# Decay attention and a hard-swish layer on one core: the exponent's bias folded into the reduction, the second layer's low weights from TensorE, and the last short unit spread over the last tile

## The chip, the cores and the metric

One core of a Trainium2 chip runs the whole program. The metric is device time in microseconds (us); lower is better. The engines are named as in the profile: PE (TensorE matmul), PEld (its weight load), DVE (VectorE), ACT (ScalarE), POOL (GpSimd) and SP (SyncE, which here issues the DMAs).

## The reference

Causal attention with a cumulative log decay for 8 batches of 8 heads (sequence 576, head size 64), then a two-layer network with a hard swish on the 4608 resulting rows (model size 512, inner size 2048), all in float32:

```python
scores = scale * np.matmul(q, k.transpose(0, 1, 3, 2))
cum = np.cumsum(np.log(np.clip(f, 0.0001, 1.0)), axis=-1)
scores = np.where(causal, -1000000000.0, scores + cum[:, :, :, None] - cum[:, :, None, :])
attn = np.exp(scores - np.max(scores, axis=-1, keepdims=True))
attn = attn / (np.sum(attn, axis=-1, keepdims=True) + 1e-09)
x = np.matmul(attn, v)          # heads side by side: 4608 x 512
h = x @ w_in                    # 512 x 2048
g = h * np.clip(h + 3.0, 0.0, 6.0) / 6.0
out = g @ w_out                 # 2048 x 512
```

## The kernel before, in words

**Precision.** Float32 products are made of float16 pieces. A matrix is scaled by a power of two and split into a high part (rounded to float16) and a low part (what is left), and a product is high x high, high x low and low x high, accumulated in PSUM. So the layers have three matmuls per block (L775 to L777 and L797 to L799 for the first, L821 to L823 for the second).

**Attention.** Batch 0 is worked on first, in pairs of heads cut at column 256 ("A" and "B" in `VH`). The 56 heads of batches 1 to 7 ("F") go through `rows`. For each of the two halves of a head's query chunks (`NAT`: three chunks, then two), `rows` computes the scores on PE into `pn` (L609, L612); DVE adds the causal mask and takes the maximum of each row in one pass (L620), writing the scores to `pp` and the maxima to `mc`; a small DVE pass turns the maxima into the exponent's bias `nb`, -max/8 + ln 16 (L626); ACT takes the exponential in place (L632), so that probabilities come out times 16 (`PSC`); ACT rounds them to float16 (L646), DVE or POOL subtract to get the low part (L649, L655, L660), and a transposing DMA brings both to `pT` (L667). `PL_POOL` and `B0_POOL` say which subtractions go to POOL: in batch 1 the chunk 3 piece of each head (L649); from batch 2 on the 64-column edges (L655, L660). `av` multiplies `pT` by the split values into `pav` (L692 to L697), and normalizes by the row sums (L721 to L727).

**POOL.** It rounds queries and keys for PE and makes their remainders (L447, L448, L456, L459).

**The layers.** A tile is 512 rows of one batch. `h_unit` makes 128 inner columns of the first layer: 12 matmuls into one PSUM bank `ph`, then ACT (L781), DVE (L784), ACT (L785) and DVE (L786) make the hard swish and its high and low part in `gT`. `out_unit` makes 128 output rows: 48 matmuls into `po`, an ACT pass (L827) and a DMA. The 64 rows by which a batch exceeds a tile are gathered for two batches into a short unit: `h_short` makes a quarter of its first layer (four groups of 128 columns, L797 to L812). For the last two batches the short unit is worked on within the last tile, in `gs`. `mm_tile` hands out the PSUM banks for all of these: two banks of the pool `ps_m`, and as every third, where its argument allows, the one bank "tr" of `ps_t`. Tile 0 comes in two parts, columns 0 to 255 and 256 to 511.

**The weights.** `w_in_work` and `w_out_work` load each weight in 16 chunks, sum its squares for a scale, and split it (`w_split`). For three of w_in's four groups the low part comes from PE: the chunk against an identity scaled by minus the scale (`eye`), plus the identity times the high part, evacuated by ACT with sign (L287 to L289). For w_out it comes from DVE (L295), which reads the float32 chunk and the high part that ACT has made (L284). The float32 of w_out's chunk k lies in the slot of `w2` that takes the parts of chunk k + 1.

**Order.** The main loop walks over `VH`; between a head's steps `fill` issues units of the layers at a rate (`F_RATE`, `even`) and `w_step` issues steps of the weights' work. That gives the program's order; the order on each engine is then made by a planner that simulates the engines with its own costs and takes the first in the program's order that it holds ready. Engines execute their queue in that order.

Of the kernel before, what the change touches and what calls it, by code (L numbers as in the profile page):

```python
# [20 lines left out]
def kernel(  # L21
# [79 lines left out]
    NSP = 3  # L101
    PL_POOL = ((3, ), ())
    NAT = ((1, 4, 0), (2, 3))
    B0_POOL = ((0, 0), (1, 1))
    W_AHEAD = (4, 5)
# [176 lines left out]
    def w_split(i, k, sc, eye=None):  # L282
        _, x, (hi, lo) = w_chunk(i, k)
        nc.scalar.activation(hi, x, AF.Copy, scale=sc)  # L284
        if eye is not None:
            pl = ps_m.tile([P, TT], F32, tag="mm", name=f"low_{k}")
            nc.tensor.matmul(pl, eye, x, start=True, stop=False)  # L287
            nc.tensor.matmul(pl, ident16, hi, start=False, stop=True)
            nc.scalar.activation(lo, pl, AF.Copy, scale=-1.0)  # L289
            return  # L290
        if POOL_REST[i][k % 4]:
            nc.scalar.activation(x, x, AF.Copy, scale=sc)
            nc.gpsimd.tensor_tensor(lo, x, hi, op=ALU.subtract)
        else:
            nc.vector.scalar_tensor_tensor(lo, x, sc, hi, op0=ALU.mult, op1=ALU.subtract)  # L295
# [29 lines left out]
    def w_out_work():  # L325
# [19 lines left out]
        for k in range(NW):  # L345
            w_split(1, k, scol(SW2 + k // NG))
            yield
# [242 lines left out]
    ringh = [t.bitcast(F16) for t in ring]  # L590

    def rows(v):
        i, j = v % NQK, v % NL
        n = VH[v][1]
        late = min(n // H, 2) - 1
        pT = p2.tile([P, 3200], F16, tag="PHL", name=f"pT_{v}")
        mc = MF[v % 2]
        nb = p2.tile([P, NCH], F32, tag="nb", name=f"nb_{v}")
        e0 = 0
        for half in range(2):  # L600
# [16 lines left out]
            for x, c in enumerate(NAT[half]):  # L617
# [3 lines left out]
                    pp[:r, w:w + kw], pn[:r, o:o + kw], W[:r, 4 * P + r - kw:4 * P + r],  # L621
                    1.0, -3.0e38, ALU.add, ALU.max, accum_out=mc[:r, e0 + x:e0 + x + 1],
                )
                w += kw
            e1 = e0 + len(NAT[half])
            nc.vector.tensor_scalar(  # L626
                nb[:, e0:e1], mc[:, e0:e1], -0.125, math.log(PSC), op0=ALU.mult, op1=ALU.add
            )
            for x, c in enumerate(NAT[half]):
                r, kw = RR[c], RB[c] + RR[c]  # L630
                x_ = pp[:r, at[c]:at[c] + kw]
                nc.scalar.activation(  # L632
                    x_, x_, AF.Exp, bias=nb[:r, e0 + x:e0 + x + 1], scale=0.125
                )
# [9 lines left out]
            for c in NAT[half]:  # L644
                r, kw, a = RR[c], RB[c] + RR[c], GH[half][c]
                nc.scalar.copy(hl[:r, h0[c]:h0[c] + kw], pp[:r, at[c]:at[c] + kw])  # L646
                if c:
                    eng = nc.gpsimd if c in PL_POOL[late] else nc.vector
                    eng.tensor_tensor(  # L649
                        hl[:r, a:a + c * P], pp[:r, at[c] + 64:at[c] + kw],  # L650
                        hl[:r, h0[c] + 64:h0[c] + kw], op=ALU.subtract,
                    )
            eng = nc.gpsimd if B0_POOL[late][half] else nc.vector
            a, b = NAT[half][:2]
            eng.tensor_tensor(  # L655
                pair(hl, h0[a] - 64, h0[b] - 64), pair(pp, at[a], at[b]), pair(hl, h0[a], h0[b]),
                op=ALU.subtract,
            )
            if 0 in NAT[half]:
                eng.tensor_tensor(  # L660
                    hl[:64, h0[0] - 64:h0[0]], pp[:64, at[0]:at[0] + 64], hl[:64, h0[0]:h0[0] + 64],
                    op=ALU.subtract,
                )
# [16 lines left out]
    def av(v, ph):  # L680
# [33 lines left out]
        for head in heads:  # L714
# [5 lines left out]
            rs = p2.tile([P, NCH, 1], F32, tag="rs", name=f"rs_{v}_{jh}")[:, p0:p1]  # L720
            nc.vector.tensor_scalar(  # L721
                rs, pav[:, p0:p1, vo + D:vo + D + 1], PSC * 1e-9, None, op0=ALU.add
            )
            nc.vector.reciprocal(rs, rs)
            if b == 0:
                nc.vector.tensor_scalar(rs, rs, scol(SV + b), None, op0=ALU.mult)
            nc.vector.tensor_tensor(  # L727
# [40 lines left out]
    def h_unit(t, fc, c0, c1):  # L768
        x = xT[t % 2]
        nw = c1 - c0  # L770
        ph = mm_tile(f"ph_{t}_{fc}_{c0}", t > 0 or c0 > 0)[:, :nw]
        fs_ = slice(fc * P, (fc + 1) * P)
# [59 lines left out]

    def moe_tile(t, c0=0, c1=TT):
        for fc in range(NFC):
            j, new = divmod(fc, NFC // NG)
            if new == 0 and c0 == 0:
                while j not in w_in_done:
                    next(w_in_q, None)
                moe_scale_in(t, j)
            yield from h_unit(t, fc, c0, c1)  # L840
        if t == 0:
            for _ in wq:
                pass
        if c0 == 0:
            moe_scale_out(t)
        last = t == B - 1
        if last:
            gs = vst.bitcast(F16).rearrange("p c e -> p (c e)")[:, 0:2 * NFC * P]
            gs = gs.rearrange("p (a f t) -> p a f t", a=2, f=NFC)
            for j in range(NG):  # L850
                yield from h_short(t // 2, j, gs)
        r0 = t * S + (64 if t else 0)
        for s in range(c0 // P, c1 // P):
            yield from out_unit(s, t > 0 or s * P >= QA, UO + t, [r0 + s * P])
        if last:
# [219 lines left out]
```

## Time and profile before

| | |
|---|---|
| median of 3 runs | 1076.95 us (1076.81 to 1079.76) |
| the profiled execution's own time | 1080.35 us |
| its span, first to last instruction | 1078.6 us |
| busy: PE, DVE, ACT, POOL | 1013.8, 726.8, 587.9, 408.5 us |
| mean granted PE clock | 0.985 |

Durations in this document come from the profiled execution; its own time is 1.75 us above its span and 3.40 us above the median. In the rows of the profile, a group of instructions is given as line, engine, operation, what it writes and reads, shapes and count, then its busy time in us and the mean ns of one, then the engine's idle time just before and which instruction ended it. Matmuls are pipelined: the duration of one includes its latency, and the distance from one start to the next is what it takes of PE. In rows of a timeline the first number is the start in us from the beginning of the span, the second the time it lasted.

### The profile page before, as it was taken

Reading aid. Unit: us, or ns where it says so; the run is one execution under the profiler, and the core shown is the slowest. Engines: PE = TensorE matmul, PEld = TensorE weight load, DVE = VectorE, ACT = ScalarE, POOL = GpSimd, SP = SyncE. Lnnn points to the kernel's source line nnn. Section 1 sums busy time; section 2 is a strip of 40 time slices with the busy share of each in tenths; the row PEclk is TensorE's granted clock in tenths of the full one; section 3 lists DMA queues with packets and bytes.
Section 4 is the critical chain, followed back from the end, with each engine's and each line's share of the span. In section 5 each row is a group of like instructions: output and inputs, shape, how many; then the busy total and the mean of one; then the engine's idle time right before and its main releaser. Section 6 shows DMA issues by size and latency. Waiting matters only on the chain.

```text
span 1078.6 us, 21257 instructions
## 1 busy us (share of the span) xinstructions
PE 1013.8 (94%) x7698; PEld 604.8 (56%) x7698; DVE 726.8 (67%) x1903; ACT 587.9 (55%) x1190; POOL 408.5 (38%) x505
## 2 busy tenths in 40 slices
PE   2799988899999999999999999999999999999897
PEld 2557854665455755555555755555555755544545
DVE  7887899887875668866865677767855678305300
ACT  4777657665664557555654547655743567315301
POOL 7434456454433445443434334443433442000000
PEclk9989989999999999999999999999999999999999
DMA  8976448965665676567465576567565554300000
GB/s 253 288 210 199 117 103 160 203 149 127 149 104 121 138 151 128 111 151 160 98 127 107 105 164 129 118 137 169 101 112 123 108 101 84 78 30 1 1 20 30
DMA packets 259300, 133.79 MB, mean 124 GB/s; under 512 B 226964, under 2 KB 228812, under 8 KB 259196
## 3 DMA queue, kind: packets, MB, share of 16 engines
q1 hardware_dynamic: 259196, 132.44, 55.7%
q8 instruction: 61, 1.00, 0.4%
q14 instruction: 43, 0.35, 0.1%
HBM read 47.93 MB, written 9.73 MB: 53 GB/s over the span
## 4 chain that ended last, share of the span: by engine, by line
PE 66%; DVE 13%; DMA 6%; ACT 6%; issue 5%; POOL 2%; SPq 1%; ACTq 0%; DVEq 0%; POOLq 0%
PE po L821 10%; PE po L822 10%; PE po L823 10%; PE ph L775 7%; PE ph L776 7%; PE ph L777 7%; DVE pp L620 3%; PE pn L609 3%; PE pn L612 3%; DMA vst<-in_vS_dram 2%; ACT pp L632 2%; DVE ring L649 2%; DVE gT L786 1%; DVE r L784 1%; DMA ring<-in_w_out_dram 1%
## 5 line engine op out<-in xcount | busy, mean ns | idle before, releaser
L632 ACT ACTIVATE pp<-pp,nb 128x192 f32<-128x192 f32 x280 | 138.9, 552 | 135.8 <-DVE nb L626 135.3
L821 PE MATMUL po<-w,gT 128*128 128x512 f16 x560 | 208.0, 383 | 5.2 <-DVE rs L809 2.8
L822 PE MATMUL po<-w,gT 128*128 128x512 f16 x560 | 210.2, 383 | 1.3 <-DVE w L295 1.3
L775 PE MATMUL ph<-xT,w 128*128 128x512 f16 (+1 forms) x576 | 201.5, 359 | 10.3 <-DVE r L784 10.1
L823 PE MATMUL po<-w,gT 128*128 128x512 f16 x560 | 210.1, 382 | 0.0
L776 PE MATMUL ph<-xT,w 128*128 128x512 f16 (+1 forms) x576 | 200.7, 358 | 0.0
L777 PE MATMUL ph<-xT,w 128*128 128x512 f16 (+1 forms) x576 | 200.0, 358 | 0.0
L649 DVE TENSOR_TENSOR ring<-pp,ring 128x128 f16<-128x128 f32 (+2 forms) x216 | 140.4, 660 | 82.6 <-ACT ring L646 81.6
L620 DVE CUSTOM_DVE_ANT_0 pp<-pn,W 128x192 f32<-128x192 f32 x280 | 123.3, 482 | 26.6 <-PE pn L612 25.0
L447 POOL TENSOR_SCALAR TK<-ST 64x576 fp32r<-64x576 f32 (+1 forms) x68 | 49.9, 733 | 240.8 <-PE pn L609 200.7
L459 POOL TENSOR_TENSOR T<-ST,T 64x576 fp32r<-64x576 f32 (+1 forms) x68 | 99.4, 1461 | 84.2 <-DMA T<-TK 72.5
L609 PE MATMUL pn<-TK,TQ 68*128 68x192 f32 x336 | 124.3, 384 | 5.0 <-issue 3.9
L784 DVE SCALAR_TENSOR_TENSOR r<-r,ph 128x512 f32<-128x512 f32 (+1 forms) x144 | 89.1, 620 | 56.2 <-ACT r L781 55.8
L785 ACT CAST gT<-r 128x512 f16<-128x512 f32 (+1 forms) x144 | 81.5, 568 | 80.8 <-DVE r L784 80.2
L786 DVE TENSOR_TENSOR gT<-r,gT 128x512 f16<-128x512 f32 (+1 forms) x144 | 103.9, 725 | 20.6 <-ACT gT L785 19.0
L781 ACT ACTIVATE r<-ph,bias_r,SC 128x512 f32<-128x512 f32 (+1 forms) x144 | 103.9, 725 | 23.1 <-PE ph L777 20.6
L646 ACT CAST ring<-pp 128x192 f16<-128x192 f32 x280 | 114.3, 449 | 0.0
L612 PE MATMUL pn<-T,T 128*128 128x192 f32 x336 | 113.0, 363 | 0.0
L456 POOL TENSOR_TENSOR T<-ST,TQ 64x576 fp32r<-64x576 f32 (+2 forms) x68 | 98.3, 1446 | 15.9 <-PE ps L552 5.4
L823 PEld LDWEIGHTS <-gT 128*128 128x128 f16 x560 | 55.0, 99 | 68.3 <-issue 9.2
L655 POOL TENSOR_TENSOR ring<-pp,ring 128x128 f16<-128x128 f32 x96 | 61.6, 642 | 80.5 <-ACT ring L646 35.2
L822 PEld LDWEIGHTS <-gT 128*128 128x128 f16 x560 | 54.9, 99 | 63.5 <-issue 8.5
(154 smaller groups left out, 1987.1 us busy)
## 6 DMA issues: line engine op xcount, KB each, us to landing
ST<-in_qk_dram SPq DMA_DIRECT2D x64, 288.0 KB
T<-TK SPq DMA_DIRECT2D x64, 144.0 KB
out_dram<-o SPq DMA_DIRECT2D x33, 256.0 KB
ring<-in_w_out_dram SPq DMA_DIRECT2D x16, 512.0 KB
T<-TQ SPq DMA_DIRECT2D x56, 144.0 KB
vst<-in_vS_dram SPq DMA_DIRECT2D x7, 1040.0 KB
ring<-in_w_in_dram SPq DMA_DIRECT2D x9, 512.0 KB
w<-in_w_in_dram SPq DMA_DIRECT2D x7, 512.0 KB
```

The lines of the kernel that those rows point to most:

```text
L609: nc.tensor.matmul(dst, TQ[i][0:D + 4, qs], TK[i][0:D + 4, a:e], start=True, stop=False)
L612: nc.tensor.matmul(dst, T7[j][:, qs], T1[j][:, a:e], start=False, stop=True)
L620: nc.vector.tensor_tensor_reduce(pp[:r, w:w + kw], pn[:r, o:o + kw], W[:r, 4 * P + r - kw:4 * P + r], 1.0, -3.0e38, ALU.add, ALU.max, accu ...
L632: nc.scalar.activation(x_, x_, AF.Exp, bias=nb[:r, e0 + x:e0 + x + 1], scale=0.125)
L649: eng.tensor_tensor(hl[:r, a:a + c * P], pp[:r, at[c] + 64:at[c] + kw], hl[:r, h0[c] + 64:h0[c] + kw], op=ALU.subtract,)
L775: nc.tensor.matmul(ph, w1[0][:, cc, fs_], xh, start=(cc == 0), stop=False)
L776: nc.tensor.matmul(ph, w1[0][:, cc, fs_], xl, start=False, stop=False)
L777: nc.tensor.matmul(ph, w1[1][:, cc, fs_], xh, start=False, stop=(cc == NCC - 1))
L786: nc.vector.tensor_tensor(gT[:, 1, fc, c0:c1], r, gT[:, 0, fc, c0:c1], op=ALU.subtract)
L821: nc.tensor.matmul(po, g[:, 0, fc, ts_], w2[:, fc, 0, c], start=(fc == 0), stop=False)
L822: nc.tensor.matmul(po, g[:, 0, fc, ts_], w2[:, fc, 1, c], start=False, stop=False)
L823: nc.tensor.matmul(po, g[:, 1, fc, ts_], w2[:, fc, 0, c], start=False, stop=(fc == NFC - 1))
```

## The change

- The reduction of L620 multiplies by -0.125 and takes the minimum, so that it writes the negative scaled scores and, for each row, the negative scaled maximum. The exponential takes that as its bias and -1 as its scale; the pass L626 is gone. Probabilities are then not times 16; the float16 copy (L646) multiplies by 16, and the subtractions do so within one pass (`low`). All the subtractions are DVE's; `PL_POOL` and `B0_POOL` are gone.
- In `av`, batch 0's scale of the values is folded into the pass that adds the small constant (L721), with its inverse, and L726 is gone.
- The low parts of w_out come from PE, as those of w_in do, through the bank "tr". `eyes` holds two scaled identities at a time, since the scale differs for each group of four chunks.
- `h_unit` and `out_unit` of tile 0 use two PSUM banks in the second part too.
- In the last tile a group of the short unit follows each second of every four `h_unit`s, where before all four came behind them.

```diff
@@ w_split
         nc.scalar.activation(hi, x, AF.Copy, scale=sc)
         if eye is not None:
-            pl = ps_m.tile([P, TT], F32, tag="mm", name=f"low_{k}")
+            pool, tag = (ps_t, "tr") if i else (ps_m, "mm")
+            pl = pool.tile([P, TT], F32, tag=tag, name=f"low_{i}_{k}")
             nc.tensor.matmul(pl, eye, x, start=True, stop=False)
             nc.tensor.matmul(pl, ident16, hi, start=False, stop=True)
             nc.scalar.activation(lo, pl, AF.Copy, scale=-1.0)
@@ w_out_work
         for k in range(NW):
-            w_split(1, k, scol(SW2 + k // NG))
+            j, new = divmod(k, NG)
+            if new == 0 and j % 2 == 0:
+                eyes = p2.tile([P, 2, P], F32, tag="junk", name=f"eyes{j}", bufs=1)
+                for i in range(2):
+                    nc.vector.tensor_scalar(
+                        eyes[:, i], identf, scol(SW2 + j + i), -1.0, op0=ALU.mult, op1=ALU.mult
+                    )
+            w_split(1, k, scol(SW2 + j), eyes[:, j % 2])
             yield
@@ rows
+    def low(out_, x, hi):
+        nc.vector.scalar_tensor_tensor(out_, x, PSC, hi, op0=ALU.mult, op1=ALU.subtract)
...
-                    1.0, -3.0e38, ALU.add, ALU.max, accum_out=mc[:r, e0 + x:e0 + x + 1],
+                    -0.125, 3.0e38, ALU.add, ALU.min, accum_out=mc[:r, e0 + x:e0 + x + 1],
                 )
                 w += kw
             e1 = e0 + len(NAT[half])
-            nc.vector.tensor_scalar(
-                nb[:, e0:e1], mc[:, e0:e1], -0.125, math.log(PSC), op0=ALU.mult, op1=ALU.add
-            )
...
-                    x_, x_, AF.Exp, bias=nb[:r, e0 + x:e0 + x + 1], scale=0.125
+                    x_, x_, AF.Exp, bias=mc[:r, e0 + x:e0 + x + 1], scale=-1.0
...
-                nc.scalar.copy(hl[:r, h0[c]:h0[c] + kw], pp[:r, at[c]:at[c] + kw])
+                nc.scalar.activation(
+                    hl[:r, h0[c]:h0[c] + kw], pp[:r, at[c]:at[c] + kw], AF.Copy, scale=PSC
+                )
                 if c:
-                    eng = nc.gpsimd if c in PL_POOL[late] else nc.vector
-                    eng.tensor_tensor(
+                    low(
                         hl[:r, a:a + c * P], pp[:r, at[c] + 64:at[c] + kw],
-                        hl[:r, h0[c] + 64:h0[c] + kw], op=ALU.subtract,
+                        hl[:r, h0[c] + 64:h0[c] + kw],
                     )
-            eng = nc.gpsimd if B0_POOL[late][half] else nc.vector
...
@@ av
-            nc.vector.tensor_scalar(
-                rs, pav[:, p0:p1, vo + D:vo + D + 1], PSC * 1e-9, None, op0=ALU.add
-            )
+            sums = pav[:, p0:p1, vo + D:vo + D + 1]
+            if b == 0:
+                nc.vector.tensor_scalar(rs, sums, PSC * 1e-9, scol(IV), op0=ALU.add, op1=ALU.mult)
+            else:
+                nc.vector.tensor_scalar(rs, sums, PSC * 1e-9, None, op0=ALU.add)
             nc.vector.reciprocal(rs, rs)
-            if b == 0:
-                nc.vector.tensor_scalar(rs, rs, scol(SV + b), None, op0=ALU.mult)
@@ h_unit
-        ph = mm_tile(f"ph_{t}_{fc}_{c0}", t > 0 or c0 > 0)[:, :nw]
+        ph = mm_tile(f"ph_{t}_{fc}_{c0}", t > 0)[:, :nw]
@@ moe_tile
             yield from h_unit(t, fc, c0, c1)
+            if last and new == 1:
+                yield from h_short(t // 2, j, gs)
...
-            for j in range(NG):
-                yield from h_short(t // 2, j, gs)
...
-            yield from out_unit(s, t > 0 or s * P >= QA, UO + t, [r0 + s * P])
+            yield from out_unit(s, t > 0, UO + t, [r0 + s * P])
```

More of the change, by code (lines that the diff above doesn't have):

```diff
@@ L101 @@
     NSP = 3
-    PL_POOL = ((3, ), ())
     NAT = ((1, 4, 0), (2, 3))
-    B0_POOL = ((0, 0), (1, 1))
     W_AHEAD = (4, 5)
@@ L594, in rows @@
         n = VH[v][1]
-        late = min(n // H, 2) - 1
         pT = p2.tile([P, 3200], F16, tag="PHL", name=f"pT_{v}")
         mc = MF[v % 2]
-        nb = p2.tile([P, NCH], F32, tag="nb", name=f"nb_{v}")
         e0 = 0
@@ L645, in rows @@
                 r, kw, a = RR[c], RB[c] + RR[c], GH[half][c]
-                nc.scalar.copy(hl[:r, h0[c]:h0[c] + kw], pp[:r, at[c]:at[c] + kw])
+                nc.scalar.activation(
+                    hl[:r, h0[c]:h0[c] + kw], pp[:r, at[c]:at[c] + kw], AF.Copy, scale=PSC
+                )
                 if c:
-                    eng = nc.gpsimd if c in PL_POOL[late] else nc.vector
-                    eng.tensor_tensor(
+                    low(
                         hl[:r, a:a + c * P], pp[:r, at[c] + 64:at[c] + kw],
-                        hl[:r, h0[c] + 64:h0[c] + kw], op=ALU.subtract,
+                        hl[:r, h0[c] + 64:h0[c] + kw],
                     )
-            eng = nc.gpsimd if B0_POOL[late][half] else nc.vector
             a, b = NAT[half][:2]
-            eng.tensor_tensor(
-                pair(hl, h0[a] - 64, h0[b] - 64), pair(pp, at[a], at[b]), pair(hl, h0[a], h0[b]),
-                op=ALU.subtract,
+            low(
+                pair(hl, h0[a] - 64, h0[b] - 64), pair(pp, at[a], at[b]),
+                pair(hl, h0[a], h0[b]),
             )
             if 0 in NAT[half]:
-                eng.tensor_tensor(
-                    hl[:64, h0[0] - 64:h0[0]], pp[:64, at[0]:at[0] + 64], hl[:64, h0[0]:h0[0] + 64],
-                    op=ALU.subtract,
+                low(
+                    hl[:64, h0[0] - 64:h0[0]], pp[:64, at[0]:at[0] + 64],
+                    hl[:64, h0[0]:h0[0] + 64],
                 )
@@ L833, in moe_tile @@
     def moe_tile(t, c0=0, c1=TT):
+        last = t == B - 1
+        if last:
+            gs = vst.bitcast(F16).rearrange("p c e -> p (c e)")[:, 0:2 * NFC * P]
+            gs = gs.rearrange("p (a f t) -> p a f t", a=2, f=NFC)
         for fc in range(NFC):
@@ L845, in moe_tile @@
             moe_scale_out(t)
[L846 to L849, printed above, removed]
-            for j in range(NG):
-                yield from h_short(t // 2, j, gs)
         r0 = t * S + (64 if t else 0)
         for s in range(c0 // P, c1 // P):
-            yield from out_unit(s, t > 0 or s * P >= QA, UO + t, [r0 + s * P])
+            yield from out_unit(s, t > 0, UO + t, [r0 + s * P])
         if last:
```

## The prediction, made before the changed kernel was run

> **What bounds the kernel now.** I read the page first (busy shares, the slices, the chain), then the busy time by stage, then who waited for whom.
>
> ```profile
> PE 1013.8 (94%) x7698; PEld 604.8 (56%) x7698; DVE 726.8 (67%) x1903; ACT 587.9 (55%) x1190; POOL 408.5 (38%) x505
> PE 66%; DVE 13%; DMA 6%; ACT 6%; issue 5%; POOL 2%; SPq 1%; ACTq 0%; DVEq 0%; POOLq 0%
> ```
>
> TensorE (PE) is busy 94% of the span and two thirds of the chain that ended last, so time is lost where PE idles or runs at a lower clock, and gained there only. Five stretches show where (columns: PE, PE weight load, DVE, ACT and POOL busy us, then the granted clock):
>
> ```profile
> 0.00:140.00 140.00, 108.67 (x698) 84.64 (x699) 114.10 (x344) 92.51 (x192) 70.34 (x88) 0.96 0.71 208
> 140.00:240.00 100.00, 84.27 (x727) 57.23 (x726) 92.75 (x260) 68.09 (x152) 57.09 (x55) 0.93 0.76 157
> 240.00:400.00 160.00, 158.02 (x1296) 92.03 (x1295) 110.28 (x283) 87.64 (x179) 65.39 (x86) 0.99 0.65 135
> 400.00:940.00 540.00, 533.92 (x4209) 302.45 (x4208) 382.53 (x980) 305.74 (x615) 215.66 (x277) 1.00 0.59 121
> 940.00:1079.00 139.00, 128.94 (x779) 68.42 (x777) 27.10 (x40) 33.91 (x53) 0.00 (x0) 0.98 0.05 16
> ```
>
> From 240 on PE is packed: 2.0 us idle to 400, 6.1 us to 940. Between 140 and 240 DVE is 93% busy and PE idles 15.7 us, at a clock of 0.93, so another 7 us of its time would be lost if it were busy throughout. I put the loss there at 20 us, since some idle time falls into the slow clock. This is where w_out is scaled and split. The waits of PE, and the longest of ACT that the change touches:
>
> ```profile
> PE ph L775 <- DVE r L784: 10.1, 9, 2.0
> ...
> PE pav L692 <- DMA pT<-ring: 4.8, 5, 2.1
> PE po L821 <- DVE rs L809: 4.6, 2, 2.8
> ...
> PE pn L609 <- issue: 3.9, 1, 3.9
> ```
>
> ```profile
> ACT pp L632 <- DVE nb L626: 135.3, 71, 4.4
> ```
>
> **Second layer's low weights on PE.** Per chunk (16 of them) L295 on DVE goes; two fp32 passes against a scaled identity, one fp16 pass against the identity and one ACT evacuation come. The same code ran for w_in:
>
> ```profile
> 62.54 1.05 PE L287 MATMUL low<-gT,eye 128*128 128x512 f32 x2
> 63.43 0.38 PE L288 MATMUL low<-w,ident 128*128 128x512 f16 x1
> 63.65 1.02 PE L287 MATMUL low<-gT,eye 128*128 128x512 f32 x2
> ```
>
> From one chunk's start to the next is 63.65 - 62.54 = 1.11 us, so PE gets 16 x 1.11 = 17.8 us more work. The rows for the other engines (groups by line; mean ns behind the busy us):
>
> ```profile
> L655 POOL TENSOR_TENSOR ring<-pp,ring 128x128 f16<-128x128 f32 x96 | 61.6, 642 | 80.5 <-ACT ring L646 35.2 <-issue 17.9 <-DVE ring L649 11.4
> ...
> L626 DVE TENSOR_SCALAR nb<-MF 128x3 f32<-128x3 f32 x112 | 43.3, 387 | 1.0
> ...
> L660 POOL TENSOR_TENSOR ring<-pp,ring 64x64 f16<-64x64 f32 x48 | 19.7, 410 | 0.1
> ...
> L295 DVE SCALAR_TENSOR_TENSOR w<-w,SC 128x512 f16<-128x512 f32 x16 | 14.6, 911 | 0.0
> ...
> L284 ACT ACTIVATE w<-w,SC 128x512 f16<-128x512 f32 x16 | 11.5, 717 | 12.3 <-DVE w L295 12.3
> ...
> L809 DVE SCALAR_TENSOR_TENSOR rs<-rs,phs 128x512 f32<-128x512 f32 x16 | 10.8, 684 | 57.1 <-ACT rs L805 56.9 <-PE phs L799 0.2
> ...
> L649 POOL TENSOR_TENSOR ring<-pp,ring 128x384 f16<-128x384 f32 x8 | 9.7, 1217 | 6.6 <-PE pn L612 4.4 <-POOL T L456 1.0 <-ACT ring L646 0.9
> ...
> L655 DVE TENSOR_TENSOR ring<-pp,ring 128x128 f16<-128x128 f32 x16 | 8.7, 543 | 0.0
> ...
> L812 DVE TENSOR_TENSOR gT<-rs,gT 128x512 f16<-128x512 f32 x12 | 8.3, 689 | 5.9 <-ACT gT L811 5.9
> ...
> L811 ACT CAST gT<-rs 128x512 f16<-128x512 f32 x12 | 7.4, 618 | 9.4 <-DVE rs L809 9.4
> L289 ACT ACTIVATE w<-low 128x512 f16<-128x512 f32 x12 | 7.0, 589 | 1.3 <-PE low L288 1.3
> ...
> L726 DVE TENSOR_SCALAR rs<-rs,SC 128x2 f32<-128x2 f32 (+1 forms) x16 | 5.9, 371 | 0.1
> ...
> L660 DVE TENSOR_TENSOR ring<-pp,ring 64x64 f16<-64x64 f32 x8 | 2.6, 325 | 0.0
> ...
> L317 DVE TENSOR_SCALAR eye<-identf,SC 128x128 f32<-128x128 f32 x3 | 1.4, 461 | 0.0
> ```
>
> DVE loses 14.6 us and gains four scaled identities, 4 x 0.46 = 1.8 us; ACT gains 16 x 0.589 = 9.4 us. All of it falls into 140 to 240. What is new is a relay. The low parts share one PSUM bank ("tr"), so a chunk's first pass waits until ACT has evacuated the chunk before; its fp16 pass waits for ACT's high part; and that high part overwrites the fp32 of the chunk before, so ACT waits there for PE. One round is 1.11 + 0.72 + 0.59, at least 2.4 us with both engines free, 39 us for 16. Before, L284 and L295 alternated in the same way, and that is the 12.3 us in L284's row. Queued behind a waiting pass on PE are the next head's scores (L609), for which DVE's reductions (L620) wait, the attention products (L692) and tile 0's output products (L821). The second pair of identities shares one buffer with the first, so DVE waits there for chunk 7's passes; one wait, 0 to 1 us.
>
> How much of the 17.8 is covered? Not at all would be +17.8; covered fully by the 20 us lost there, -2. DVE drops from 93 by 14.6 - 1.8 and the changes below to about 80, so its lateness, the reason of the 3.9 us gap and of the po waits, mostly goes. But ACT rises from 68 to 77 with the heads' pace set by PE and ACT together, and PE would need 84 + 18 of 100 us. I take 12.5 us of the 20 as recovered; some waits on transposes (L692) and on the relay stay. Net +5.3.
>
> **Exponent's bias.** 112 small DVE passes go (43.3 us) and with them the reason of ACT's 135.3 us of waiting; each exponential now waits for its own reduction alone. The reduction has the same form with other constants. ACT's copy gets a constant scale: with a per-partition scale the pass takes 717 ns (L284), a plain cast 618 (L811), with a constant 589 (L289, from PSUM). Bounds: 0 to 0.1 us each for the 280 copies of the 56 heads, 0 to 28 us of ACT; about ten heads lie between 140 and 240, five copies each, so at the upper end ACT would reach 82 of 100 there and I would take 1.5 us less as recovered. I take 0, because L289 is the nearest. The Trainium skill, "ScalarE: Activation LUTs", section "What ACT_TABLE_LOAD costs", says the same thing by a rule: a constant scale is free and each per-partition operand adds about 93 ns; the trace agrees (717 against 618). By that rule the copies add nothing, and ACT as the bound of the split stage is that much less likely.
>
> The subtractions become multiply-and-subtract passes: at one shape 684 (L809) against 689 (L812), so no change. Those of POOL move to DVE, at the means there of L655 and L660 and POOL's own for L649: 96 x 0.543 + 48 x 0.325 + 8 x 1.217 = 77 us. The median of L655 on DVE is shorter (min/median/max ns):
>
> ```profile
> L655 DVE TENSOR_TENSOR ring<-pp,ring x16: 274/280/1497, 149.9 to 229.5; 128x128 f16<-128x128 f32 x16
> ```
>
> With 0.28 the sum is 52 us. Against 43.3 + 14.6 + 5.9 - 1.8 = 62 us removed, DVE ends between 717 and 742 us, 66 to 69% of the span. In the packed stages that is not a bound, so this costs nothing. If DVE came late it would show as ph waits (10.1 us now). POOL's 91 us less lets its copies for later heads and the DMAs behind them start earlier, in queues that have room; the transposes on SP's queue are issued sooner, none is added or moved. The folding of L726 saves 5.9 us of DVE off the path.
>
> The gain is that ACT, no longer idle for nb, runs L781 sooner, so DVE frees ph sooner. Of the 6.1 us of PE idle from 400 to 940 I take 3.5 as recovered, and 1 of those 240 to 400 (0 to all of each as bounds).
>
> **Two banks instead of three for tile 0's second part.** The units of 256 columns, half of which ran on two banks already, show this:
>
> ```profile
> L775 PE MATMUL ph<-xT,w 128*128 128x256 f16 x128 | 35.0, 279 | 2.9 <-DVE r L784 2.7
> ```
>
> 2.7 us of waits for all 32 units. Bounds for the 16 that change and the two output units: 0 to 9 (half a microsecond a unit); I take +1, from that row.
>
> **Last short unit spread.** Its four groups ran in one block behind the last tile's first layer, and one of them just ahead of the end:
>
> ```profile
> 1015.31 0.58 PE L821 MATMUL po<-w,gT 128*128 128x512 f16 x1 [2.80 <-DVE rs L809]
> ```
>
> ```profile
> 1066.86 0.27 PE L821 MATMUL po<-w,vst 128*128 128x256 f16 x1 [1.83 <-DVE rs L809]
> ```
>
> ```profile
> 1000.00:1020.00 20.00, 17.20 (x180) 11.85 (x179) 7.84 (x12) 8.07 (x15) 0.00 (x0) 0.91 0.00 1
> ```
>
> PE waits 2.80 and 1.83 us for their evacuation, and behind the first runs at a lower clock (0.91 of 20 us, 1.8 us lost). Spread over the tile, each evacuation lies beside the next units' PE work: DVE and ACT are there at 27 and 34 us of 139. Saved 6.4 at most, nothing if the planner still puts one last; I take 6.
>
> **Sum.** 17.8 - 12.5 - 3.5 - 1 + 1 - 6 = -4.2 us, against the profiled execution of 1080.35 us (span 1078.6). That stands 3.4 us above the median of 1076.95, so I forecast 1072.7 us.
>
> **Rivals.** (1) Slower: the relay between PE and ACT holds up PE's queue. The split now takes 53 us, 3.3 a chunk:
>
> ```profile
> L295 DVE SCALAR_TENSOR_TENSOR w<-w,SC x16: 704/739/1905, 139.0 to 191.7; 128x512 f16<-128x512 f32 x16
> ```
>
> If that stays, PE idles much as before: recovery 4 rather than 12.5, and 2.5 us rather than 4.5 from the two middle terms. The sum is 17.8 - 4 - 2.5 + 1 - 6 = +6.3, 1083. It speaks for it that the round is 2.4 us bare and ACT also carries two exponential groups a head; against it, that scores and products of other heads are ready to fill PE. It decides once recovery falls below 8 us. (2) Full cover: with PE's gaps filled the clock stays up between 140 and 240 and at 280; recovery 18 to 20, the sum -10 to -12, 1066. The Trainium skill, "TensorE: Matmul & The Clock Gate", section "What's actually happening", has the rule that a PE idle for a window of about 3.4 us falls to half speed and needs as long a busy one to return; the trace agrees in kind, its clock being lowest, 0.93, in the stage with the 3.9 us gap. (3) The bias pass was not what made ph late: in the packed stages, where PE has 6.1 us to win, DVE takes over POOL's pieces and stays as late as it was, so the 4.5 us there stay lost. The sum is +0.3, 1077. For it speaks that DVE's time hardly changes; against it that ACT's longest wait is the one removed.
>
> **Chances.** My forecast (-8 to -1) 0.46, rival 1 0.20, rival 2 0.15, rival 3 0.19. A difference under 0.3% (3.2 us) is about what this kernel's measurement cannot tell from none. Faster: 0.8 of the first and all of rival 2, 0.52; same: the rest of the first and 0.8 of rival 3, 0.24; slower: 0.24. Own range of the forecast 1069 to 1076; the range over all cases reaches from full cover's middle to somewhat past rival 1: 1063 to 1085.
>
> **What would show it.** L626 and the DVE form of L295 gone and ACT's wait for L632 far below 135 us; PE's idle time from 140 to 240 under 10 us with the clock above 0.95; no wait of L821 for L809 after 1000; POOL near 317 us; the copies of L646 no longer than now. I am wrong if L287's new passes wait for ACT by more than a few us in total, if ph waits for L784 grow past 10 us, or if the stage to 240 ends later by more than 6 us.

## The result, and the profile after

The kernel after takes 1130.69 us (median; 1130.13 to 1141.02), beside 1077.73 us for the kernel before on the same chip: a ratio of 1.0511 (95% interval 1.0449 to 1.0574). The forecast was 1072.7 us, with 1063 to 1085 as its range. The change makes the kernel 5% slower; of the 53 us, most are lost between 130 and 400 us, and they start in one stretch of 56 us.

The busy row of the page after (us, share of the span of 1128.3 us, instructions):

```profile
PE 1038.9 (92%) x7746; PEld 622.1 (55%) x7746; DVE 711.7 (63%) x1915; ACT 608.2 (54%) x1206; POOL 326.3 (29%) x353
```

PE's idle time is 1128.3 - 1038.9 = 89.4 us, before it was 64.8; its busy time grew by 25.1 us, of which the new passes are some 17 and the rest, as an estimate, goes to a lower granted clock (0.976, before 0.985). The stages after, in the columns of those before:

```profile
140.00:240.00 100.00, 75.09 (x477) 49.95 (x475) 44.78 (x127) 47.67 (x96) 26.14 (x26) 0.88 0.34 76
240.00:400.00 160.00, 143.65 (x1145) 86.27 (x1144) 129.34 (x352) 92.46 (x194) 67.12 (x62) 0.96 0.73 153
400.00:940.00 540.00, 537.46 (x4340) 310.57 (x4339) 375.54 (x1020) 317.50 (x624) 172.18 (x185) 1.00 0.61 127
```

The first row is the surprise. I had expected DVE to come down to 80 of 100 us and PE to be full; every engine fell: DVE from 93 to 45, ACT from 68 to 48, POOL from 57 to 26, PE from 84 to 75, in spite of its added work. All engines emptier at once means that something holds up the program, not that one engine is the bound. The waits of DVE from 130 to 260 us (us in total, times, longest) name it:

```profile
DVE junk L497 <- PE low L286: 28.9, 1, 28.9
DVE eyes L349 <- PE low L286: 26.1, 1, 26.1
```

Two single waits, 55 us together, on the new passes. In the timeline of DVE (start, duration) nothing else runs in between:

```profile
130.24 0.14 DVE L392 COPY SC<-SC 64x1 f32<-64x1 f32 x1
156.49 0.48 DVE L349 TENSOR_SCALAR eyes<-identf,SC 128x128 f32<-128x128 f32 x2 [26.11 <-PE low L286]
185.82 0.69 DVE L497 CUSTOM_DVE_ANT_0 junk<-pn,W 128x512 bf16<-128x512 f32 x1 [28.85 <-PE low L286]
```

The reduction of `natural` for batch 0's last head (L497 after, L491 before) writes its scores to a scratch buffer, "junk", of which there is one. The change puts the scaled identities `eyes` into the same buffer. The second pair waits until chunks 0 to 7 have used the first, and the reduction waits until chunks 8 to 15 have used the second. The two rows of that line, before and after (min/median/max ns, first and last start):

```profile
L491 DVE CUSTOM_DVE_ANT_0 junk<-pn,W x40: 270/546/750, 14.1 to 119.0; 128x128 bf16<-128x128 f32 x8, 128x256 bf16<-128x256 f32 x8, 128x512 bf16<-128x512 f32 x8, 128x384 bf16<-128x384 f32 x8
```

```profile
L497 DVE CUSTOM_DVE_ANT_0 junk<-pn,W x40: 269/551/750, 14.2 to 187.2; 128x128 bf16<-128x128 f32 x8, 128x256 bf16<-128x256 f32 x8, 128x512 bf16<-128x512 f32 x8, 128x384 bf16<-128x384 f32 x8
```

The last maxima come at 187 us instead of 119. Without them the head has no scores, POOL does not get its buffers back, and no later head starts; PE has nearly nothing but tile 0's output products and the split. POOL's wait for the scores (the longest 72.3 us):

```profile
POOL TK L453 <- PE ps L555: 81.8, 5, 72.3
```

Why the split takes 56 us shows in one round of it, PE first, then ACT:

```profile
140.76 1.02 PE L286 MATMUL low<-w,eyes 128*128 128x512 f32 x2
141.62 0.38 PE L287 MATMUL low<-w,ident 128*128 128x512 f16 x1
143.13 0.38 PE L826 MATMUL po<-w,gT 128*128 128x512 f16 x1 [1.14 <-ACT w L288]
...
144.43 1.02 PE L286 MATMUL low<-w,eyes 128*128 128x512 f32 x2
```

```profile
141.88 0.72 ACT L282 ACTIVATE w<-w,SC 128x512 f16<-128x512 f32 x1 [2.46 <-PE low L286]
142.51 0.58 ACT L288 ACTIVATE w<-low 128x512 f16<-128x512 f32 x1
```

From pass to pass it is 144.43 - 140.76 = 3.67 us. PE's pass (1.02), ACT's next high part (0.72, since it overwrites what the pass reads) and ACT's low part (0.58) follow one another, and then come six matmuls of the second layer that use this very chunk (143.13 to 144.43, 1.30 us), which PE has in its queue ahead of the next chunk. The parts end up strictly in series.

PE pays for this series directly too. In 15 of the 16 rounds the first of the six matmuls stands until ACT has written the low part, 15.0 us in all; PE's idle time grew by 24.6 us altogether (PE's two longest waits from 130 to 260 us):

```profile
PE po L826 <- ACT w L288: 15.0, 15, 1.1
PE pn L616 <- issue: 6.7, 1, 6.7
```

The late heads go on costing after the split. From 200 to 220 us the granted clock is 0.50, and from 240 to 400 PE idles 16.3 us, where before it idled 2.0:

```profile
200.00:220.00 20.00, 13.32 (x62) 12.04 (x63) 18.03 (x54) 10.65 (x24) 11.54 (x12) 0.50 0.39 89
```

### The profile page after: what moved, and what is told of

It reads as the page before. It is cut to its first block, busy times and chain, and to the rows that moved or that the text cites. A ratio compares the mean times of both kernels' runs of the same rounds, so it can differ in the third digit from the quotient of the medians.

```text
span 1128.3 us, 20886 instructions
## 1 busy us (share of the span) xinstructions
PE 1038.9 (92%) x7746; PEld 622.1 (55%) x7746; DVE 711.7 (63%) x1915; ACT 608.2 (54%) x1206; POOL 326.3 (29%) x353
## 4 chain that ended last, share of the span: by engine, by line
PE 69%; DVE 14%; DMA 6%; ACT 6%; issue 3%; POOL 2%; SPq 1%; ACTq 0%; DVEq 0%; POOLq 0%
PE po L826 11%; PE po L825 11%; PE po L827 11%; PE ph L779 7%; PE ph L780 6%; PE ph L781 6%; DVE ring L599 3%; PE pn L619 3%; PE pn L616 3%; DVE pp L627 2%; DMA vst<-in_vS_dram 2%; PE low L286 2%; DVE r L788 2%; DMA TQ<-mr 1%; DVE gT L790 1%
## 5 line engine op out<-in xcount | busy, mean ns | idle before, releaser
L826 PE MATMUL po<-w,gT 128*128 128x512 f16 x560 | 209.0, 380 | 15.0 <-ACT w L288 15.0
L779 PE MATMUL ph<-xT,w 128*128 128x512 f16 (+1 forms) x576 | 201.7, 360 | 14.3 <-DVE r L788 11.4
L599 DVE SCALAR_TENSOR_TENSOR ring<-pp,ring 128x128 f16<-128x128 f32 x392 | 177.8, 492 | 52.3 <-ACT ring L650 50.3
L636 ACT ACTIVATE pp<-pp,MF 128x192 f32<-128x192 f32 x280 | 148.4, 554 | 93.7 <-DVE MF L627 92.8
L465 POOL TENSOR_TENSOR T<-ST,T 64x576 fp32r<-64x576 f32 (+1 forms) x68 | 102.7, 1512 | 152.6 <-DMA T<-TK 148.9
L453 POOL TENSOR_SCALAR TK<-ST 64x576 fp32r<-64x576 f32 (+1 forms) x68 | 54.0, 794 | 318.0 <-PE pn L616 219.0
L650 ACT ACTIVATE ring<-pp 128x192 f16<-128x192 f32 x280 | 121.1, 459 | 1.8 <-DMA pT<-ring 0.2
L826 PEld LDWEIGHTS <-gT 128*128 128x128 f16 x560 | 54.8, 98 | 67.2 <-issue 12.2
L780 PEld LDWEIGHTS <-w 128*128 128x128 f16 x576 | 56.7, 98 | 61.5 <-issue 20.5
```

The costliest lines, as they stand in the source:

```text
L599: nc.vector.scalar_tensor_tensor(out_, x, PSC, hi, op0=ALU.mult, op1=ALU.subtract)
L636: nc.scalar.activation(x_, x_, AF.Exp, bias=mc[:r, e0 + x:e0 + x + 1], scale=-1.0)
L650: nc.scalar.activation(hl[:r, h0[c]:h0[c] + kw], pp[:r, at[c]:at[c] + kw], AF.Copy, scale=PSC)
L779: nc.tensor.matmul(ph, w1[0][:, cc, fs_], xh, start=(cc == 0), stop=False)
L780: nc.tensor.matmul(ph, w1[0][:, cc, fs_], xl, start=False, stop=False)
L826: nc.tensor.matmul(po, g[:, 0, fc, ts_], w2[:, fc, 1, c], start=False, stop=False)
```

## The experiments

Letters used in the expectations: A is the identity buffer shared with the reductions; B the passes and their relay with ACT as a cost by themselves; C the rest of the change; D any one-at-a-time thing that the passes share with other work. For what remains without the passes, P is the subtractions moved to DVE, Q the two banks, F the folded bias, S the scaled forms of copy and subtraction; O is the order that the planner happens to write, and W the work itself, whatever its order. "tr" is the single PSUM bank, "mm" the pair. In the edits shown, "..." stands for lines left out.

**e1: identities in a buffer of their own** (after, one line changed).

```diff
-                eyes = p2.tile([P, 2, P], F32, tag="junk", name=f"eyes{j}", bufs=1)
+                eyes = p2.tile([P, 2, P], F32, tag="eyes", name=f"eyes{j}", bufs=2)
```

> The changed kernel, but the scaled identities have a buffer of their own (tag eyes, two deep) rather than the one they share with the scratch of the first batch's row maxima (tag junk, one deep). Theory A, the shared buffer: the 55 us for which DVE stood behind it (26.1 us before the second pair of identities, 28.9 us before the last maxima) go, the split spreads out again, 1075 to 1088 us. Theory B, the relay: with one PSUM bank for the low parts each chunk still takes about 3.7 us of PE's queue and all else stands behind it; at most 15 us come back, above 1112 us. Theory C, the rest of the change (bias, subtractions, two banks) is what costs: no better than 1115 us.

1128.46 us (1126.18 to 1129.07), ratio 1.0495 (1.0474 to 1.0515). The two waits are gone, and one of the same length is there, for the transposed maxima of `max_rows`, which need the bank "tr" in which the passes go round:

```profile
DVE mr L508 <- PE ptm L506: 55.1, 1, 55.1
```

A alone is refuted: there are two shared things, and the bank is enough by itself.

**e2: the low parts in the bank pair** (after; identities still in "junk").

```diff
-            pool, tag = (ps_t, "tr") if i else (ps_m, "mm")
+            pool, tag = ps_m, "mm"
```

> The changed kernel, but the low parts of w_out go through the two mm banks rather than the one bank tr; the identities still share the buffer junk. Theory A: the order of identities and maxima on DVE is as before, its two long waits stay at 40 us or more together, 1110 to 1135 us. Theory B: two banks break the relay, the round falls from 3.7 us to 2.5 or less, 1085 to 1105 us. Theory C: 1120 to 1135 us.

1110.41 us (1106.82 to 1114.61), ratio 1.0326 (1.0294 to 1.0358). With two banks the split is over in 21 us, ahead of the output products:

```profile
L286 PE MATMUL low<-w,eyes x32: 592/592/697, 132.6 to 152.6; 128*128 128x512 f32 x32
```

DVE's waits for `eyes` and `junk` are 10.0 and 9.6 us now. So whoever shares waits as long as the split lasts. Neither A nor B fits whole: the waits are not A's 40 us or more, and the time is not B's 1085 to 1105.

**e3: the low parts of w_out on DVE again** (after, with that edit undone).

```diff
...
-            w_split(1, k, scol(SW2 + j), eyes[:, j % 2])
+            w_split(1, k, scol(SW2 + k // NG))
```

> The changed kernel with one part undone: the low parts of w_out come from DVE again, everything else as changed. Theories A and B: the whole loss is in that part, 1068 to 1080 us. Theory C: 1105 us or more.

1096.9 us (1091.65 to 1100.15), ratio 1.0195 (1.016 to 1.0229). The low parts bring 34 of the 53 us; some 20 us are elsewhere.

**e4: the low parts alone** (before with that edit, and the two banks that it needs).

```diff
...
-            w_split(1, k, scol(SW2 + k // NG))
...
+            w_split(1, k, scol(SW2 + j), eyes[:, j % 2])
```

> The kernel before with that one part done: low parts of w_out from PE through tr, identities in junk, tile 0 on two banks. Theories A and B: the loss comes back, 1118 to 1140 us. Theory C: below 1100 us.

1136.81 us (1131.05 to 1137.91), ratio 1.0559 (1.0528 to 1.0591), with the same two waits. By itself, with these banks, the part costs some 60 us, more than the whole change, so the costs of the parts don't add up:

```profile
DVE junk L499 <- PE low L288: 28.9, 1, 28.9
DVE eyes L351 <- PE low L288: 26.0, 1, 26.0
```

**e5: as e1, and the transposed maxima in "mm".**

```diff
-        pt = ps_t.tile([P, 512], F32, tag="tr", name=f"ptm_{v}")
+        pt = ps_m.tile([P, 512], F32, tag="mm", name=f"ptm_{v}")
```

> e1 (identities in their own buffer) and also the transpose of the row maxima (ptm) moved from the bank tr to an mm bank, so that nothing of the first batch's last head shares a buffer with the low parts. Theory D: either shared thing alone puts that head's maxima behind all 16 chunks, so with both gone DVE no longer stands for 55 us, 1080 to 1105 us (what e3 showed, about 20 us over the kernel before, may stay). Theory B, PE's queue itself is full of the relay: above 1115 us.

1112.6 us (1111.85 to 1115.48), ratio 1.0333 (1.0298 to 1.0367). The 55 us wait is gone, 16 us of time with it; the time lies between D's range (up to 1105) and B's (from 1115). Now a third user of "tr" waits, the scale of the next batch's values:

```profile
DVE e_v L185 <- PE pt_v L182: 23.4, 1, 23.4
```

**e9: as e5, and that scale in "mm" too.**

```diff
-        pool, tag = (ps_t, "tr") if SV < s_col < SV + B else (ps_m, "mm")
+        pool, tag = ps_m, "mm"
```

> The kernel after, with the identities in a buffer of their own and both the transposed maxima (ptm) and the reduction of the next batch's values (pt_v) in the bank mm, so that no other user of the bank tr is left ahead of the low passes in this stretch. Theory D (any user of a thing that the 16 passes hold one at a time stands behind all 16): no wait of DVE of over 15 us on ptm or pt_v between 130 and 240 us, the time at the level of the kernel after with the low weights on DVE again (1097), say 1085 to 1102; the split itself may still go at 3.67 us a chunk without costing anything beyond its own PE work. Theory B (the relay between PE and ScalarE costs by itself, whoever shares the bank): 16 rounds of 3.67 us with some 1.1 us of stalled PE each are still there and the time stays near 1112, with PE's waits in 140 to 240 us as large as in the run with two of the sharers taken out.

1113.6 us (1111.24 to 1114.95), ratio 1.0328 (1.0296 to 1.036), and the wait is still 24.4 us: a miss for D as I had put it, and what B foretold. The timeline of PE shows why it decides nothing:

```profile
211.37 0.38 PE L826 MATMUL po<-w,gT 128*128 128x512 f16 x1 [0.69 <-ACT w L288]
211.59 0.38 PE L827 MATMUL po<-w,gT 128*128 128x512 f16 x1
211.80 0.38 PE L826 MATMUL po<-w,gT 128*128 128x512 f16 x1
212.02 0.38 PE L827 MATMUL po<-w,gT 128*128 128x512 f16 x1
212.74 0.38 PE L182 MATMUL pt_v<-vm,ones 128*128 128x1 f32 x2 [0.35 <-ACT o L831]
```

Six output matmuls a round are two sums `po`, one in each bank of "mm", and each holds its bank until the last chunk. I had moved the scale from one queue behind the split to another; it starts as soon as ACT has read a sum out. PE's wait for ACT's low parts (L826) is 6.8 us here and in e5, where it was 15.0.

**e12: before, with the low parts on PE in "mm" and identities of their own**; the third bank stays.

```diff
-            w_split(1, k, scol(SW2 + k // NG))
...
+                eyes = p2.tile([P, 2, P], F32, tag="eyes", name=f"eyes{j}", bufs=2)
...
+            w_split(1, k, scol(SW2 + j), eyes[:, j % 2])
```

> The kernel before with the low weights of the second layer made on PE, in the bank pair mm and with identities in a buffer of their own, so that no maxima share anything that the passes hold one at a time; the third bank stays as before. Theory D: the split takes about 20 us, DVE has no wait of over 10 us in 130 to 200 us, and the time is 1077 plus at most the 17.8 us of added PE work less what DVE's 25 us are worth there: 1068 to 1092. Theory B (PE work and relay in this stretch cost whatever is shared): 1095 or more.

1090.69 us (1089.41 to 1093.89), ratio 1.0122 (1.0089 to 1.0155). DVE's longest wait from 130 to 260 us is 6.6 us, and PE's output products no longer wait for ACT's low parts. The split was expected to take about 20 us; it takes 45:

```profile
L287 PE MATMUL low<-w,eyes x32: 592/593/1057, 139.5 to 183.9; 128*128 128x512 f32 x32
```

Though the split is long, no wait of DVE stands behind it. Page and stage:

```profile
PE 1029.4 (95%) x7746; PEld 611.6 (56%) x7746; DVE 711.0 (65%) x1891; ACT 596.3 (55%) x1206; POOL 406.5 (37%) x505
```

```profile
140.00:240.00 100.00, 88.97 (x698) 57.39 (x697) 66.65 (x196) 66.69 (x144) 38.44 (x42) 0.98 0.59 123
```

This is nearly the stage as I had forecast it: PE fuller (11.0 us idle, forecast under 10), at 0.98, DVE relieved. PE's idle time is 1087.5 - 1029.4 = 58.1 us, 6.7 less than before; busy time is 15.6 more. Between these two profiles the split without the sharing nets +8.9 us of span, where the sum had +5.3; by the medians it is +12.9 (1090.69 against 1077.78), since the profile of before is one of its slower executions.

**e8: the spread of the last short unit alone** (before with that edit).

```diff
+            if last and new == 1:
+                yield from h_short(t // 2, j, gs)
...
```

> The kernel before with only the last short unit spread over the last tile. In the changed kernel PE still waits 2.3, 2.3 and 0.9 us in the last tile against 2.8 and 1.8 before, so a gain of 0 to 3 us: 1073 to 1077 us. My first account (the waits go) says 1070 us.

1080.89 us (1077.94 to 1084.15), ratio 1.0029 (1.0009 to 1.0048): nothing gained, rather 3 us lost. All waits of PE from 980 to 1079 us:

```profile
PE ph L775 <- DVE r L784: 2.1, 1, 2.1
PE po L821 <- DVE r L784: 2.1, 1, 2.1
PE po L821 <- ACT o L827: 0.8, 1, 0.8
```

5.0 us, before 4.6. The waits for the short unit are gone and as long ones for the full unit have come: in ACT's order the short unit's pass stands ahead of a full unit's pass and stalls for its input,

```profile
1013.17 0.56 ACT L805 ACTIVATE rs<-phs,bias_r,SC 128x256 f32<-128x256 f32 x1 [5.71 <-PE phs L799]
1013.64 1.44 ACT L781 ACTIVATE r<-ph,bias_r,SC 128x512 f32<-128x512 f32 x2
```

**e6 and e7: the other parts alone** (before with `rows` and `av` of the change; before with the two banks in tile 0's second part).

```diff
-            nc.vector.tensor_scalar(
-                nb[:, e0:e1], mc[:, e0:e1], -0.125, math.log(PSC), op0=ALU.mult, op1=ALU.add
-            )
...
-                    eng = nc.gpsimd if c in PL_POOL[late] else nc.vector
-                    eng.tensor_tensor(
+                    low(
...
```

> The kernel before with only the exponent's bias folded, all subtractions on DVE, and L726 folded. Theory P, what e3 still lost lies here (DVE takes POOL's pieces in the stage from 140 to 260 us, where it is full, and the queues are planned anew): 1085 to 1100 us. Theory Q, it lies in the two banks: 1066 to 1078 us.

```diff
-        ph = mm_tile(f"ph_{t}_{fc}_{c0}", t > 0 or c0 > 0)[:, :nw]
+        ph = mm_tile(f"ph_{t}_{fc}_{c0}", t > 0)[:, :nw]
...
```

> The kernel before with only the second part of tile 0 on two PSUM banks. Theory P: 1074 to 1080 us, no difference. Theory Q: 1085 us or more.

e6 takes 1093.33 us (1091.7 to 1099.99), ratio 1.016 (1.0115 to 1.0205); e7 1088.14 us (1086.66 to 1090.98), ratio 1.0104 (1.0068 to 1.0139). Read by themselves, both parts cost more than ten microseconds; P had foretold e6 and Q e7, and each missed the other. In e6 PE waits for POOL's remainders from 130 to 260 us, which before it did not:

```profile
PE pn L613 <- POOL T L459: 11.9, 6, 4.7
```

**e10 and e11: e6 taken apart.** e10 folds the bias and keeps the subtractions on their engines; e11 only gives POOL's subtractions to DVE.

```diff
-                    eng = nc.gpsimd if c in PL_POOL[late] else nc.vector
-                    eng.tensor_tensor(
+                    low(
+                        nc.gpsimd if c in PL_POOL[late] else nc.vector,
...
```

> The kernel before with the exponent's bias folded into the masking reduction, but the remainders of the probabilities subtracted on the engines they were on (part of them on POOL); left out: the factor of 16 on the packed heads' probabilities and on the small constant of their sums. Theory P (the fold alone is worth a little or nothing; what costs in the run with the whole of this change, +16 us, is the subtractions taken from POOL to DVE): 1070 to 1079, no wait of PE on TK's transfer over 6 us near 200 us. Theory F (the fold itself, its longer pass order or the reduction's other form, costs): 1088 to 1096, with the same waits of PE at POOL's T (11.9 us) and at ScalarE's w.

```diff
-    PL_POOL = ((3, ), ())
+    PL_POOL = ((), ())
-    B0_POOL = ((0, 0), (1, 1))
+    B0_POOL = ((0, 0), (0, 0))
```

> The kernel before with the subtractions that POOL makes of the probabilities' remainders given to DVE, nothing else. Theory P: 1088 to 1098, and the waits at POOL's T and at w appear. Theory F: 1076 to 1080.

e10: 1078.76 us, ratio 1.0007 (0.9984 to 1.003). e11: 1077.23 us, ratio 1.0002 (0.9982 to 1.0023). Neither half costs anything; together they had cost 16 us. P and F are refuted as I had put them. What is left: the scaled forms, which both halves leave out, or the order that the planner writes.

**e16: both halves together without the scaled forms** (the edits of e10 and e11), in nearly e6's order, and **e13 to e15: another order and next to no other work** (before, e6 and e7, each with this one pass made twice).

```diff
             nc.vector.tensor_scalar(e[:, 0:1], pt[:, 0:1], 2.0 ** -100, None, op0=ALU.max)
+            nc.vector.tensor_scalar(e[:, 0:1], pt[:, 0:1], 2.0 ** -100, None, op0=ALU.max)
```

> The kernel before with a pass of one column on DVE made twice, wherever a power-of-two scale is worked out (13 places, about 0.15 us each, 2 us of DVE in all); the planner's order changes on every engine (on PE in some 6% of the rows). Theory O (which order the planner happens to write is worth ten microseconds or more in the stage to 260 us): the time leaves that of the kernel before by more than 4 us, to either side. Theory W (the work counts, not the order): 1074 to 1080.

> The run with the whole of the bias change alone (1093), with the same doubled pass of one column, so that it has another order. Theory O: away from 1093 by more than 4 us, most likely down towards 1080, and PE's 11 us of waiting for POOL's T gone or elsewhere. Theory W: 1090 to 1097 with the waits for POOL's T as they were.

> The run with two banks in tile 0 alone (1088), with the same doubled pass. Theory O: away from 1088 by more than 4 us. Theory W (two banks cost 10 us by themselves): 1085 to 1091.

> The bias folded in, all the subtractions on DVE, but as plain subtractions and with a plain copy for the high part; left out: the factor of 16 on the packed heads' probabilities. Its order on PE, POOL and SP is nearly that of the run with the whole of this change (20 of 14,044 rows on PE differ). Theory O: like that run, 1088 to 1097, since fold alone and subtractions on DVE alone each left the time where it was, and the order is what they share. Theory S (the scaled forms, copy and multiply-and-subtract, are what costs the 16 us): 1075 to 1081.

e16: 1091.71 us (1086.81 to 1094.68), ratio 1.0113 (1.0067 to 1.016), with 11.4 us of waiting for POOL's remainders as in e6: the scaled forms are not the cause. e13: 1097.22 us (1094.24 to 1100.08), ratio 1.0169 (1.0123 to 1.0214): **2 us of DVE work and another order make the kernel before 20 us slower.** e14: 1086.83 us, ratio 1.0081 (1.0057 to 1.0106), 6 us better than e6; e15: 1100.9 us, ratio 1.0196 (1.0141 to 1.0251), 13 us worse than e7. What O had foretold came out in all four, though e14, 9 us above before, keeps more than half of e6's loss, and its wait for POOL's remainders is halved (6.1 us) rather than gone. Page and first two stages of e13:

```profile
PE 1028.2 (94%) x7698; PEld 614.0 (56%) x7698; DVE 728.1 (66%) x1916; ACT 589.3 (54%) x1190; POOL 409.8 (37%) x505
```

```profile
0.00:140.00 140.00, 105.80 (x620) 79.83 (x621) 104.73 (x311) 89.70 (x185) 58.94 (x80) 0.91 0.68 198
140.00:240.00 100.00, 83.72 (x644) 60.30 (x644) 84.11 (x242) 58.76 (x127) 53.45 (x49) 0.85 0.64 136
```

Most of the loss is in the first 240 us: the clock there is 0.91 and 0.85 where it was 0.96 and 0.93. Over the whole span the same matmuls take 14.4 us longer, and 5.3 us of idle time are added.

**e17: the whole change, mended** (after, with the low parts in "mm" and identities of their own), and **e18: the change unmended, in another order** (after with the doubled pass).

> The kernel after with the low parts of w_out in the two banks mm and the identities in a buffer of their own; the rest of the change as it is. Theory D (what the change loses is what the 16 passes hold one at a time): the split takes 20 to 45 us, no wait of DVE of over 12 us between 130 and 240, and the time falls from 1131 to the run with the low weights back on DVE (1097) or below: 1085 to 1105, the width being what another order is worth (20 us). Theory B (the passes on PE cost whatever they share): 1108 or more.

> The kernel after with the doubled pass of one column that gives another order. Theory D (program order and one buffer, which no order of the planner can get around): DVE still stands over 20 us at the second identities and at the first maxima behind them, and the time is 1120 to 1145. Theory O alone (the 54 us are an unlucky order): it falls below 1110 and the two waits are gone.

e17: 1097.5 us (1097.15 to 1100.0), ratio 1.0184 (1.0157 to 1.021). e18: 1134.99 us (1133.41 to 1140.67), ratio 1.0533 (1.0499 to 1.0567), and DVE's two waits are there as before, to 0.2 us:

```profile
DVE junk L498 <- PE low L287: 28.9, 1, 28.9
DVE eyes L350 <- PE low L287: 26.3, 1, 26.3
```

D holds in both: e17's longest wait of DVE from 130 to 260 us is 11.3 us, and it stands at a first-layer pass. With e1 and e2 this makes a square: 1131 us with both shared things, 1128 with the bank alone (e1), 1110 with the identity buffer alone (e2), 1097 with neither. So the bank alone costs 31 us, the buffer alone 13, and both together 33: the buffer adds little to the bank, as the same head's maxima stand behind either. Of the bank's 31 us, 16 went with the maxima (e5). The remaining 15, from e5 and e9 to e17, went only with the pair of banks, which takes away the sharing and the one-bank relay together; no run tells these two apart, so B is refuted for passes in the pair, and open for passes in one bank.

The other 20 us of the change are no more than what e13 lost to an order, which does not show that an order is their cause. The eleven versions without the low parts on PE (before, e3, e6 to e8, e10, e11, e13 to e16) lie between 1077 and 1101 us. No version was measurably faster than the kernel before.

## Why the prediction was wrong, point by point

- **The failed step.** "The second pair of identities shares one buffer with the first, so DVE waits there for chunk 7's passes; one wait, 0 to 1 us." I had the wait and its cause; its size was 26.1 us, since DVE asks for the second pair as soon as it has made the first, while chunk 7 comes half a split later. And I did not look for who else uses that buffer: the reductions, another 28.9 us. The bank "tr" I named, but only as shared by the chunks with each other; its other users, the maxima and the values' scale, each stand behind all 16 passes (e1, e5). What is queued behind these waits on DVE is the rest of the attention. So the term "I take 12.5 us of the 20 as recovered" failed with it: from 140 to 240 us PE's idle time rose from 15.7 to 24.9 us and its clock fell from 0.93 to 0.88. With the pair of banks and identities of their own (e17) the change takes 33 us less, which is still above the range.
- **Rival 1** had the right sign and a part of the mechanism: the relay does hold up PE's queue, by 15.0 us, seen not on the new passes, where the prediction had said to look, but on the output products behind them (L826). Its round, "at least 2.4 us", lacked the six output matmuls between two chunks: 2.4 + 1.3 = 3.7, measured 3.67. The length of the split was nearly right (56 us against 53). What the rival did not have is who stood behind the split: "scores and products of other heads", the argument held against it, could not fill PE, since those heads had no maxima. Hence 53 us and not its +6.3.
- **The 17.8 us of PE work** were right: 0.86 us from pass to identity pass (141.62 - 140.76), and 0.22 for that one, are 1.08 a chunk, 17.3 in all. The 12.5 us were not to be seen in the change; in e12, without the sharing, idle time and clock recover part of the 20 us, with +8.9 us net by the profiles and +12.9 by the medians against the +5.3 forecast. Whether that is the work or the order can't be told, as an order is worth more than the difference.
- **Subtractions on DVE, "this costs nothing"**: right (e11, 1.0002). They were forecast to keep DVE busy for 52 to 77 us more; in e11 its busy time rose by 20.5 us (747.3, before 726.8).
- **Copies with a constant scale, "I take 0"**: right; 10 ns each, before and after:

```profile
L646 ACT CAST ring<-pp 128x192 f16<-128x192 f32 x280 | 114.3, 449 | 0.0
```

```profile
L650 ACT ACTIVATE ring<-pp 128x192 f16<-128x192 f32 x280 | 121.1, 459 | 1.8 <-DMA pT<-ring 0.2
```

- **"Of the 6.1 us of PE idle from 400 to 940 I take 3.5 as recovered."** The stage row after has 2.5 us idle, 3.5 recovered to the tenth, but that is luck in part: the window lies by the clock, so a later kernel has other work in it, and over all profiles of this study PE is busy 533.9 to 536.2 us there in the eight without the fold and 534.0 to 538.2 in the twelve with it, 1.5 us more on the mean. ACT's wait for the bias did not go; it moved to the reduction itself, 92.8 us where it was 135.3. e10, which folds the bias and leaves the subtractions where they were, has 2.4 us idle from 400 to 940 and none from 240 to 400 (before 6.1 and 2.0), the gain forecast, and yet the same time, since from 140 to 240 its idle time is 22.9 us, before 15.7. With the subtractions on DVE as well, e6 idles 5.4 and 3.8 us in the two later stages, which is nearly what rival 3 said. Which of the two holds beyond these orders stays open.
- **Two banks, "+1 (0 to 9)"**: e7 against before says +11; e15 against e13, in another order, +4, which is not clear of the noise. Both are within what an order is worth; left open.
- **Spread, "I take 6"**: nothing (e8; PE's waits there are 5.0 us, before 4.6). My proviso, "nothing if the planner still puts one last", looked at where the last group goes; the loss came from the planner putting a group's ACT pass ahead of a ready one in the middle of the tile.
- **The frame of the sum.** Terms of mostly 1 to 6 us were added to the time of one order as if the order stayed. The text had a planner that rewrites every queue, and no term and no range for that. e13 shows 20 us for it, nearly as much as all the gains claimed together (12.5 + 3.5 + 1 + 6 = 23). The kernel before is at the low end of the orders seen, so an edit had, by these runs, more to lose than to win by its order.

## What to carry to other kernels

Before work that goes round a one-deep buffer or bank many times is put into it, list every other user of it in the program's order: each stands behind the whole series, so its delay is rounds x length of a round, not one round, and what counts is what that user holds up. When all engines get emptier in the same stage, look for one long single wait rather than for a bound. And where a planner writes the queues, measure what an edit without work does to the time before claiming or blaming a few microseconds for one with work.

## What was not expected of the hardware

Gaps of a few microseconds can cost PE more in clock than in idle time: e13 has 5.3 us more idle time than before and 14.4 us more busy time for the same 7698 matmul records, at a mean granted clock of 0.970 against 0.985. One such gap in e13, with PE idle for 2.65 us up to 144.55 and busy throughout from 146 (us, PE busy, then as in the stages; the granted clock is the third number from the end):

```profile
142.00:144.00 2.00, 0.00 (x0) 0.00 (x0) 2.00 (x5) 0.00 (x0) 2.00 (x2) 0.99 0.20 20
146.00:148.00 2.00, 2.00 (x11) 1.63 (x10) 1.77 (x11) 1.24 (x3) 0.32 (x1) 0.50 0.00 0
154.00:156.00 2.00, 2.00 (x7) 1.08 (x7) 1.58 (x5) 0.63 (x2) 0.00 (x0) 0.50 0.16 39
158.00:160.00 2.00, 2.00 (x13) 1.23 (x13) 1.95 (x8) 0.07 (x1) 1.23 (x2) 1.00 0.02 5
```

The clock was half for more than ten microseconds of work. The Trainium skill, "TensorE: Matmul & The Clock Gate", section "What's actually happening", says that full speed comes back only after a whole busy window of about 3.4 us. The trace of before agrees: behind the 3.9 us gap that ends at 153.6 us its clock is 0.50 from 154 to 158 and 0.94 in the next 2 us. In e13 the return took about three times as long as that window, and no run here shows why.
